# Spectral mixer: the filter's turned sums move from VectorE to accumulating transfers between rows

## The chip, the cores and the metric

The kernel runs on one core of a Trainium2 chip. The metric is the time of one launch on the device, in microseconds (us); lower is better. Five engines work side by side: TensorE (PE in the profile; its weight loads are PEld), VectorE (DVE), ScalarE (ACT), GpSimd (POOL) and SyncE (SP). SP and POOL start most of the transfers here; each works through its own list in order.

## The reference

```python
def _A_ref(x, w_r, w_i):                      # a filter in the frequency domain
    X = jnp.fft.rfft2(x, axes=(-2, -1)) * (w_r + 1j * w_i)
    return jnp.fft.irfft2(X, s=(S, D), axes=(-2, -1))

def _B_ref(x, w1, b1, w2, b2):                # an MLP over the token axis
    h = _layernorm(x, axis=-1)
    u = _gelu(jnp.einsum("bsd,sf->bdf", h, w1) + b1)
    y = jnp.einsum("bdf,fs->bds", u, w2) + b2
    return y.transpose(0, 2, 1)

xn = _layernorm(x, axis=-1)
return x + _A_ref(xn, A_w_r, A_w_i) * _silu(_B_ref(xn, B_w1, B_b1, B_w2, B_b2))
```

Here S = 2048 tokens, D = 512 channels and F = 1792 hidden units, all in float32.

## The kernel before, in words

The rows are cut into 16 blocks of 128 (`NJ`), the hidden units into 14 blocks of 128 (`NF`). A float32 factor is split into a high and a low part, and a product is made of three matmuls (`mm3`): high by high, high by low, low by high. The high part is a ScalarE copy, the low part a VectorE subtraction (`split`, `high_low`).

**The first stage** (to 99.4 us) runs over the 16 row blocks: layernorm, seven of the hidden blocks (in seven PSUM banks), and the filter's first transform, folded into `ey`.

**The middle stage** does two things in turns. One is the other seven hidden blocks, in two batches over the 16 row blocks: 32 parts of `w1` in all, part `i` with four blocks of hidden units where `i` is under 16 and with three above (`BATCHES`, `w1_part`, `hidden_rest`). Six parts are prepared in the first stage (`w1_early`). Of the others, those in `ADDED` (10, 12, ... 20) get their low part without VectorE: ScalarE writes minus the high part, and an accumulating transfer on POOL's queue (`accum_op=ALU.add`) adds `w1` to it once more. The other thing is the filter, eight pairs of frequency groups in the order 1, 2, 0, 3, 4, 5, 6, 7 (`filter_pair(n)`, called o0 to o7 here by place). A pair goes through these steps:

1. `gf` is loaded; eight matmuls by `cd` and a ScalarE copy to `sh`.
2. Eight matmuls of 64x512 (`ps<-sh,gf`), the pair's spectrum in PSUM. ScalarE copies it to `here` (half of `xc`, two copies, L540). Four transfers on SP's queue put into `there`, the other half, the rows of the partner frequency (rows r and r+32 change places, L543).
3. VectorE makes the two turned sums, `here` plus or minus `there` with the row's sign (L561, L562), and multiplies by the filter's weights `wt` (two of 128x1024, L565). `wt` comes by POOL's queue into three buffers (`WT`), so that its loads wait for L565 of the pair before.
4. VectorE adds and subtracts the products (L567 to L569) and puts in the edge columns (L570).
5. 64 small matmuls (`ps<-hf,xc`) transform back; ScalarE copies the result to `ey` (L586).

`PACE` and `LAST` are written out by hand: how many steps of the hidden blocks (three matmuls of 128x512) stand between the filter's steps on TensorE. The step-5 matmuls of pair k come ahead of the step-2 matmuls of pair k+2, so that a pair has about two pair periods from one to the other. TensorE's order is kept as written (`Kept`); the other engines' orders are set by a scheduler, unless an instruction is wrapped in `keep`. Between the filter's steps stand the `forms` of the hidden units: sums and high/low splits for the last stage.

**The last stage** multiplies by `w2` with seven products in place of eight (`ORDER`, `w2_forms`), does the filter's last transform (`channels`, `spectral`), the gate (L789) and the sum into the output.

Of the kernel before, what the change touches and what calls it, by code (L numbers as in the profile page):

```python
# [8 lines left out]
F32 = mybir.dt.float32  # L9
# [20 lines left out]
ADDED = range(10, 22, 2)  # L30
# [21 lines left out]
def _constants():  # L52
# [29 lines left out]
    g = np.zeros((P, 8, 2, 2, 32))  # L82
# [3 lines left out]
    for lo in range(16):  # L86
        for hi in range(4):
            k1, (n, l), (t, h) = 16 * hi + lo, divmod(lo, 2), divmod(hi, 2)
            for r in range(16):
# [15 lines left out]
                p = l * 64 + h * 16 + r, l * 64 + 32 + h * 16 + r  # L105
                for s in range(2):
                    g[rows, n, l, s, h * 16 + r] = back[n, t, p[s], 0] = out[s, rows]
                    freq[p[s], n, t] = k[s]
# [11 lines left out]
        "c_h": back.reshape(16, P, 2, 64).astype(np.float32),  # L120
# [15 lines left out]
def spectral_mixer_kernel(tc, x, w1, b1, w2, b2, wk, we, wx, c_f, c_ft, c_d, c_i, c_g, c_h, out):  # L136
# [14 lines left out]
    with tc.tile_pool(name="ps", bufs=1, space=PSUM) as psp, ExitStack() as left, ExitStack() as right:  # L151
# [9 lines left out]
        for row in range(0, P, 32):  # L161
            sign = 1.0 if row % 64 else -1.0
            G.memset(turn[row:row + 32, 0:1], sign)
            G.memset(turn[row:row + 32, 1:2], -2.0 * sign)
# [14 lines left out]
        w1p = pool(lstage, "left", "w1", 4)  # L179
        lnp = pool(rstage, "right", "ln", 2)  # L180
# [86 lines left out]
        def w1_load(j, f0, nf, up, wide):  # L267
            raw = up.tile([P, wide * P], F32, name=f"w1r{f0}_{j}", tag="w1r", bufs=3)
            SY.dma_start(raw[:, :nf * P], w1[:, j, f0 * P:(f0 + nf) * P])
            return raw[:, :nf * P]  # L270
# [21 lines left out]

        def gelu(ft, bank):
# [3 lines left out]
            A.activation(raw[i][:, half], ps[:, bank], AF.Gelu_apprx_tanh, bias=b1t[:, ft:ft + 1])  # L297

        def high_low(tile, k, src):

            t = tile.rearrange("p k (a c) -> p k a c", a=2)[:, k]
            A.activation(t[..., 0, :], src, AF.Copy)
            V.tensor_sub(t[..., 1, :], src, t[..., 0, :].bitcast(F32))  # L303
# [5 lines left out]
        def forms(i):  # L309
            u = raw[i].rearrange("p a (b c) -> p (a b) c", b=2)  # L310
# [5 lines left out]
            high_low(d[0], d[1], u[:, 2])  # L316
            form[i] = {1: (d[0], d[1])}
            yield
            a = held_tile(f"fa{i}")
            high_low(a, slice(0, 2), u[:, 0:2])  # L320

            V.tensor_sub(u[:, 1], u[:, 1], u[:, 3])
            V.tensor_sub(u[:, 3], u[:, 2], u[:, 3])
            V.scalar_tensor_tensor(u[:, 2], u[:, 1], -1.0, u[:, 2], op0=ALU.mult, op1=ALU.subtract)
            V.scalar_tensor_tensor(u[:, 0], u[:, 2], -1.0, u[:, 0], op0=ALU.mult, op1=ALU.subtract)
            form[i].update({2: (a, 0), 3: (a, 1)})
            yield
            b, c = held_tile(f"fb{i}"), held_tile(f"fc{i}")
            high_low(c, slice(0, 2), u[:, 2:4])
            high_low(b, slice(0, 2), u[:, 0:2])  # L330
            form[i].update({4: (b, 0), 7: (b, 1), 6: (c, 0), 5: (c, 1)})
# [7 lines left out]
        BATCHES = ((((4, 2), (10, 2)), (7, 2, 0, 1)), (((6, 1), (12, 2)), (7, 0, 1)))  # L339
        w1_early, pairs = {}, {}  # L340

        def w1_runs(i, where, queue, **how):
            f = 0
            for f0, nf in BATCHES[i // NJ][0]:
                queue.dma_start(where[:, f:f + nf * P], w1[:, i % NJ, f0 * P:(f0 + nf) * P], **how)  # L345
                f += nf * P

        def w1_early_load(i):
            if i % 2 == 0:
                pairs[i // 2] = usp.tile([P, 2, D], F32, name=f"w1e{i}", tag="u")  # L350
            w1_runs(i, pairs[i // 2][:, i % 2], SY)
# [58 lines left out]
        for j in range(NJ):  # L410
# [10 lines left out]
            if j == 4:  # L421
                SY.dma_start(cd, c_d)
                G.dma_start(cft, c_ft)
            if j in (6, 8, 10, 12):
# [48 lines left out]

        def w1_part(i):
# [3 lines left out]
            j, (runs, _) = i % NJ, BATCHES[i // NJ]  # L478
            n = sum(r[1] for r in runs) * P
            w = w1p.tile([P, 4 * P], F32, name=f"w1s{runs[0][0]}_{j}", tag="w1r", bufs=3)[:, :n]  # L480
            w1_runs(i, w, SY)
# [403 lines left out]
```

## Time and profile before

| | |
|---|---|
| median of 3 runs | 388.89 us (388.51 to 389.69) |
| the profiled execution | 389.42 us, of which 387.6 us are the span of the profile |
| busy: TensorE, VectorE, ScalarE, POOL | 373.5, 317.4, 227.0, 85.5 us |
| moved by transfers | 69.81 MB, mean 180 GB/s |
| granted TensorE clock | 0.994 |

The profile is of one execution. Its own time is 0.5 us above the median, and 1.8 us of it lie outside the span. A row of a timeline gives start, duration, engine, line, operation, tiles and shape; in brackets stands the idle time of the engine just before it, and what ended that. POOL's rows for a transfer are the time of issuing it. A DMA "share" is the time that packets took, over 16 DMA engines.

### The profile page before, as it was taken

What the parts mean: (1) busy time and instruction counts of PE and PEld (TensorE: products, weight loads), DVE (VectorE), ACT (ScalarE), POOL (GpSimd) and SP (SyncE); (2) the same over time, 40 slices, a digit from 0 to 9 for tenths busy, and PEclk for the clock granted to TensorE, in tenths of its full rate; (3) what the DMA queues carried; (4) which work ended last, traced back from release to release, by engine and by line L of the source; (5) the groups of instructions that cost most, each with busy time, mean ns of one, the idle gap of its engine ahead of it and who ended that gap; (6) DMA issues with size and microseconds to landing.
All of it is one profiled execution on the core that took longest, in us unless ns stands there. A gap on an engine that the chain in (4) does not pass through costs nothing.

```text
span 387.6 us, 7793 instructions
## 1 busy us (share of the span) xinstructions
PE 373.5 (96%) x2872; PEld 328.1 (85%) x2872; DVE 317.4 (82%) x671; ACT 227.0 (59%) x411; POOL 85.5 (22%) x147
## 2 busy tenths in 40 slices
PE   7999999999999999999799889999999999999993
PEld 3888888888877777777588889999999999999992
DVE  5899999976549999778996898796969787878871
ACT  4676767754853555575427794655656565646441
POOL 2133233221504444422101003030302020201100
PEclk9999999999999999999999999999999999999997
DMA  8974687312835699988739298997969697876502
GB/s 257 290 262 150 230 275 256 96 55 68 245 95 160 169 268 261 220 234 218 199 94 225 58 261 201 246 183 194 192 159 218 141 222 133 221 147 163 84 1 54
DMA packets 37062, 69.81 MB, mean 180 GB/s; under 512 B 5136, under 2 KB 20896, under 8 KB 36896
## 3 DMA queue, kind: packets, MB, share of 16 engines
q1 hardware_dynamic: 28512, 48.13, 40.7%
q0 software_dynamic: 8512, 21.18, 28.3%
q8 instruction: 22, 0.36, 0.4%
q14 instruction: 16, 0.13, 0.1%
HBM read 60.91 MB, written 8.13 MB: 178 GB/s over the span
## 4 chain that ended last, share of the span: by engine, by line
PE 82%; DVE 5%; DMA 4%; ACT 3%; issue 2%; SPq 2%; POOL 0%; DVEq 0%; ACTq 0%; POOLq 0%
PE ps L823 33%; PE ps L378 20%; PE ps L133 18%; PE ps L242 4%; PE ps L758 3%; DMA s<-in_w_dram 3%; DMA xc<-xc 2%; PE ps L367 2%; PE ps L148 1%; PE ps L147 1%; PE ps L149 1%; ACT w2f L701 1%; SPq L543 1%; DVE xc L565 1%; SPq L345 1%
## 5 line engine op out<-in xcount | busy, mean ns | idle before, releaser
L378 PE MATMUL ps<-h,w1h 128*128 128x512 f32 x224 | 58.7, 398 | 0.0
L133 PE MATMUL ps<-h,w1h 128*128 128x512 f32 x152 | 48.8, 402 | 0.0
L702 DVE TENSOR_TENSOR w2f<-s,w2f 128x896 fp32r<-128x896 f32 x32 | 34.8, 1092 | 16.7 <-ACT w2f L701 16.1
L378 PEld LDWEIGHTS ps<-h,w1h 128*128 128x128 f32 x224 | 40.9, 188 | 7.9
L823 PE MATMUL ps<-fa,w2f 128*128 128x256 f32 x336 | 43.4, 282 | 0.0
L823 PE MATMUL ps<-fc,w2f 128*128 128x256 f32 x336 | 41.7, 280 | 1.6 <-DVE fc L303 0.7
L823 PE MATMUL ps<-fb,w2f 128*128 128x256 f32 x336 | 42.6, 281 | 0.1
L823 PEld LDWEIGHTS ps<-fa,w2f 128*128 128x128 f32 x336 | 41.6, 188 | 0.8
L823 PEld LDWEIGHTS ps<-fc,w2f 128*128 128x128 f32 x336 | 40.3, 188 | 2.2 <-DVE fc L303 0.9
L823 PEld LDWEIGHTS ps<-fb,w2f 128*128 128x128 f32 x336 | 40.5, 188 | 0.5 <-DVE c L793 0.5
L692 POOL DMA_DIRECT2D s<-in_w_dram x16 | 13.9, 870 | 122.3 <-DVE es L763 42.2
L701 ACT ACTIVATE w2f<-s 128x896 fp32r<-128x896 f32 x32 | 30.1, 949 | 15.1 <-DVE s L715 11.0
L133 PEld LDWEIGHTS ps<-h,w1h 128*128 128x128 f32 x152 | 27.2, 188 | 9.8 <-issue 4.9
L702 DVE TENSOR_TENSOR w2f<-a,w2f 128x896 fp32r<-128x896 f32 x24 | 26.1, 1086 | 8.6 <-ACT w2f L701 8.6
L378 PE MATMUL ps<-h,w1l 128*128 128x512 f32 x112 | 30.6, 389 | 0.0
L701 ACT ACTIVATE w2f<-a 128x896 fp32r<-128x896 f32 x24 | 22.8, 951 | 12.6 <-PE ps L823 7.7
L133 PE MATMUL ps<-h,w1l 128*128 128x512 f32 x76 | 29.7, 390 | 0.0
L378 PEld LDWEIGHTS ps<-h,w1l 128*128 128x128 f32 x112 | 21.0, 188 | 4.6
L799 POOL DMA_DIRECT2D out_dram<-g x15 | 13.6, 904 | 43.9 <-DVE g L797 28.4
L373 DVE TENSOR_TENSOR w1l<-w1r,w1h 128x512 fp32r<-128x512 f32 (+1 forms) x32 | 20.7, 648 | 2.4 <-ACT w1h L370 2.2
L597 POOL DMA_DIRECT2D wt<-in_wk_dram x16 | 10.3, 645 | 49.6 <-DVE xc L565 49.0
L823 PE MATMUL ps<-fd,w2f 128*128 128x256 f32 x168 | 21.2, 279 | 0.0
(129 smaller groups left out, 769.4 us busy)
## 6 DMA issues: line engine op xcount, KB each, us to landing
a<-in_w_dram SPq DMA_DIRECT2D x24, 448.0 KB, 3.9
s<-in_w_dram SPq DMA_DIRECT2D x16, 448.0 KB, 4.1
s<-in_w_dram POOLq DMA_DIRECT2D x16, 448.0 KB, 6.6
wt<-in_wk_dram POOLq DMA_DIRECT2D x16, 384.0 KB, 4.9
w1s<-in_w_dram SPq DMA_DIRECT2D x36, 128.0 KB, 3.3
w1r<-in_w_dram SPq DMA_DIRECT2D x16, 256.0 KB, 3.7
xc<-xc SPq DMA_DIRECT2D x32, 128.0 KB, 3.2
x<-in_x_dram SPq DMA_DIRECT2D x15, 256.0 KB, 3.9
```

What stands on the lines that cost most here:

```text
L133: return lambda *args, **kw: self.keep(operation(*args, **kw))
L242: T.matmul(z[:, b], h[:, b * P:(b + 1) * P], c, start=True, stop=True)
L367: T.matmul(ps[:, 0], wz[:, :P], wz, start=True, stop=True)
L373: keep(V.tensor_sub(dst, src, hi.bitcast(F32)))
L378: T.matmul(ps[:, bank + i], w[wi][:, i * P:(i + 1) * P], hj, start=first and j == 0, stop=last and j == NJ - 1)
L597: G.dma_start(wt[:, :3], wk[:, i, 1:])
L692: G.dma_start(t, w2_half(*added), accum_op=ALU.add)
L701: A.activation(wf[:, 0], v, AF.Copy)
L702: V.tensor_sub(wf[:, 1], v, wf[:, 0].bitcast(F32))
L758: T.matmul(pe[:, b % 2, b // 2], yt[:, b], ci[:, b], start=True, stop=True)
L799: G.dma_start(out[:, j, cols], g[:, cols], accum_op=ALU.add)
L823: T.matmul(o, wf[:, wi, i], ui, start=m + a == 0 and n in (1, 2, 5), stop=m == NH - 1 and a == 2, skip_group_check=n in (6, 3, 7, 4))
```

## The change

In the filter, the spectrum is now laid out so that partner frequencies lie in neighbouring rows. ScalarE copies it three times (six copies of 128x512 a pair): times the row's sign into a new tile `tx` (with one buffer), and as it is and with a minus into the two halves of `xc`. Two accumulating transfers on POOL's queue, of 64 rows each, then add the neighbour's row of `tx` to both halves. So VectorE makes no turned sum. The product with `wt` is cut into four of 128x512, and the edge columns take one small operation more. The order of transfers on POOL's queue is fixed: a `wt`, the two accumulating transfers, the next `wt`; `wt` is one transfer in place of two, and so is `hf`.

No `w1` part is made by accumulation: all 26 go through `split`. Raw parts are loaded into pools of their own, up to two or three buffers ahead (`w1_ahead`, `AHEAD`). `turn` is loaded and not made by memsets. At the seam of the middle and last stages the order is written out by hand (`step`, `last_sum`, `form_a` to `form_d`): the first two `w2` tiles are loaded by POOL and split ahead of the last three hidden blocks, and the forms of hidden units 5 and 6 are put between these.

```diff
             xc = mp.tile([P, 2, 2, 2, 256], F32, name=f"xc{n}", tag="xc")
-            there, here = xc[:, 0], xc[:, 1]
+            tx = mp.tile([P, 2, 2, 256], F32, name=f"tx{n}", tag="tx", bufs=1)
+            minus, here = xc[:, 0], xc[:, 1]
...
+            def copies(to, scale):
+                for t in range(2):
+                    A.activation(to[:, :, t].rearrange("p s (g c) -> p g s c", c=64), signals(ps[:, 6 - t]), AF.Copy, scale=scale)
+
+            copies(tx[:, ::-1], turn[:, 1:2])
+            copies(here, 1.0)
+            copies(minus, -1.0)
...
+            wt = wts.pop(), weights(2 * n + 1)
+            for c in range(2):
+                turned_rows = tx[1 - c::2].rearrange("p s t c -> p (s t c)").unsqueeze(1).broadcast_to([64, 2, 2 * D])
+                keep(G.dma_start(xc[c::2].rearrange("p k s t c -> p k (s t c)"), turned_rows, accum_op=ALU.add))
+            if n != order[-1]:
+                wts.append(weights(2 * order[order.index(n) + 1]))
+            yield
+            s1 = mp.tile([P, 3, 2, 2], F32, name=f"s1_{n}", tag="s1")
+            k1, k2 = (e[:, 2 * n:2 * n + 2].rearrange("p t s -> p s t") for e in (e1, e2))
+            V.tensor_mul(s1[:, 0], tx[:, ::-1, :, 0], k2)
+            V.scalar_tensor_tensor(s1[:, 1], tx[:, ::-1, :, 0], turn[:, 0:1], here[:, :, :, 0], op0=ALU.mult, op1=ALU.add)
+            V.tensor_mul(s1[:, 2], s1[:, 1, ::-1], k1)
             for t in range(2):
-                A.activation(here[:, ::-1, t].rearrange("p s (g c) -> p g s c", c=64),
-                             ps[:, 6 - t].rearrange("p (g s c) -> p g s c", s=2, c=64), AF.Copy)
-            for to, of in ((0, 32), (32, 0), (64, 96), (96, 64)):
-                SY.dma_start(there[to:to + 32], here[of:of + 32])
+                V.tensor_mul(here[:, :, t], here[:, :, t], wt[t][:, ::3])
+                V.tensor_mul(minus[:, :, t], minus[:, :, t], wt[t][:, 1:3])
+            yield
+            V.tensor_add(minus, minus, here[:, ::-1])
+            V.tensor_sub(here[:, 0], minus[:, 1], minus[:, 0])
+            V.tensor_add(here[:, 1], minus[:, 1], minus[:, 0])
+            V.tensor_add(here[:, :, :, 0], s1[:, 0], s1[:, 2])
...
-            V.scalar_tensor_tensor(av, bv[:, ::-1], turn[:, 0:1], av, op0=ALU.mult, op1=ALU.add)
-            V.scalar_tensor_tensor(bv, bv, turn[:, 1:2], av[:, ::-1], op0=ALU.mult, op1=ALU.add)
-            for t in range(2):
-                v = xc.rearrange("p k s t c -> p (k s) t c")[:, :, t]
-                V.tensor_mul(v, v, wt[t])
...
         def weights(i):
             wt = mp.tile([P, 4, 256], F32, name=f"wt{i}", tag="wt", bufs=WT)
-            G.dma_start(wt[:, :3], wk[:, i, 1:])
-            G.dma_start(wt[:, 3], wk[:, i, 0])
+            keep(G.dma_start(wt, wk[:, i]))
...
-            if i in ADDED:
-                A.activation(wh, w, AF.Copy)
-                A.activation(wl, wh.bitcast(F32), AF.Copy, scale=-1.0)
-                w1_runs(i, wl, G, accum_op=ALU.add)
-                return wh, wl
             split(wh, wl, w)
...
+        nxt = {"a12": w2_load("a12", w2p, 0, 1, queue=G), "a11": w2_load("a11", w2p, 0, 0, queue=G)}
+        in_order.append(True)
...
         ready = [next(wforms), next(wforms)]
-        run(rest)
-        for steps in zip(forms(5), forms(6)):
-            pass
+        last_sum(12, 1, 0)
+        gelu(12, 0)
+        form_d(5)
+        form_a(5)
+        sums(5)
+        last_sum(13, 2, 1)
+        gelu(13, 1)
+        form_d(6)
+        last_sum(6, 0, 7)
+        form_c(5)
+        form_b(5)
+        ready.append(next(wforms))
+        gelu(6, 7)
+        form_a(6)
...
```

On ScalarE, in the middle stage, this stands around the copies of o3 and o4 (pairs 3 and 4) before. `xc_1766` and `xc_1889` are the two pairs' `xc`, `w1h` and `w1l` a part's high and low half; a row's bracket lists the semaphores it waits for (DMAHW: a transfer started by SP, DMASW: one started by POOL).

```order
L540 ACTIVATE xc_1766<-ps 128x4x2x64 [waits DMAHW1_49,DMAHW2_49,DMAHW0_49,DMAHW3_49,DVE_49,PE_49]
L540 ACTIVATE xc_1766<-ps 128x4x2x64 [waits PE_49]
L484 ACTIVATE w1h_12_1782<-w1s_12_1779 128x512 [waits PE_49]
L485 ACTIVATE w1l_12_1783<-w1h_12_1782 128x512 [waits PE_49,Activation_49]
L144 ACTIVATE w1h_13_1824<-w1s_13_1821 128x512 [waits DMAHW4_49,DMAHW3_49,PE_49]
L525 ACTIVATE sh_0_1819<-ps 128x512 [waits PE_49]
L525 ACTIVATE sh_1_1838<-ps 128x512 [waits PE_49]
```

And now, at the same place (`tx_1770` and `xc_1769` are those of o3):

```order
L582 ACTIVATE tx_1770<-ps,turn 128x4x2x64 [waits DMASW0_49,DVE_49,DMASW7_49,PE_49,Activation_49]
L582 ACTIVATE tx_1770<-ps,turn 128x4x2x64 [waits PE_49]
L582 ACTIVATE xc_1769<-ps 128x4x2x64 x4
L145 ACTIVATE w1h_1786<-w1s_1670 128x512 [waits DMAHW4_49,DMAHW3_49,PE_49]
L145 ACTIVATE w1h_1823<-w1s_1709 128x512 [waits DMAHW6_49,DMAHW5_49,PE_49]
L560 ACTIVATE sh_0_1821<-ps 128x512 [waits PE_49,Activation_49]
L560 ACTIVATE sh_1_1847<-ps 128x512 [waits PE_49,Activation_49]
```

Two copies have become six, and the first of them waits for two transfers that POOL started: those that accumulate from `tx` for the pair before, since `tx` has one buffer.

On POOL's queue, around the same pairs, before (`wt` in two transfers each, and the accumulating transfers of w1 parts 12 and 14):

```order
L597 DMA wt_1717<-in_wk_dram 128x768
L598 DMA wt_1717<-in_wk_dram 128x256
L597 DMA wt_1773<-in_wk_dram 128x768
L598 DMA wt_1773<-in_wk_dram 128x256
L345 DMA w1l_12_1783<-in_w_dram 128x256 x2
L597 DMA wt_1840<-in_wk_dram 128x768
L598 DMA wt_1840<-in_wk_dram 128x256
```

And now (`xc_1769` is o3's, `xc_1897` o4's):

```order
L643 DMA wt_1655<-in_wk_dram 128x1024
L643 DMA wt_1777<-in_wk_dram 128x1024
L598 DMA xc_1769<-tx_1770 64x2x1024 x2
L643 DMA wt_1781<-in_wk_dram 128x1024
L643 DMA wt_1905<-in_wk_dram 128x1024
L598 DMA xc_1897<-tx_1898 64x2x1024 x2
```

Each pair's two accumulating transfers, of 512 KB each, now stand behind a load of `wt` that waits for VectorE's products of the pair before.

More of the change, by code (lines that the diff above doesn't have):

```diff
@@ L104, in _constants @@
                 rows = slice(64 * t, 64 * t + 64)
-                p = l * 64 + h * 16 + r, l * 64 + 32 + h * 16 + r
+                p = [l * 64 + 2 * (h * 16 + r) + c for c in range(2)]
                 for s in range(2):
-                    g[rows, n, l, s, h * 16 + r] = back[n, t, p[s], 0] = out[s, rows]
+                    g[rows, n, l, h * 16 + r, s] = back[n, t, p[s], 0] = out[s, rows]
                     freq[p[s], n, t] = k[s]
@@ L472, in spectral_mixer_kernel, with w1_ahead @@
             folds = fold(j, first_copy(j, z))
+        loaded = {}
+        w1_stage = ExitStack()
+        w1_raw = []
+        def w1_ahead(i):
+            n = BATCHES[i // NJ][1] * P
+            if i == NJ:
+                w1_stage.close()
+                w1_raw[0] = pool(lstage, "left", "w1b", 3)
+            loaded[i] = w1_raw[0].tile([P, n], F32, name=f"w1s{i}", tag="w1s")
+            last = w1_runs(i, loaded[i])
+            if i == 2 * NJ - 1:
+                keep(last)
         def w1_part(i):
@@ L615, in hidden_rest @@
         def hidden_rest():
-            w = w1_parts
+            w, ahead = w1_parts, list(range(NE, 2 * NJ))
             for i in range(2 * NJ):
```

195 lines of the change are left out of this document (105 added, 90 removed).

## The prediction, made before the changed kernel ran

> **What bounds the kernel now.** I read first the page's busy times and its slices, then TensorE's waits, then TensorE's timeline around the filter, then the other engines there.
>
> ```profile
> PE 373.5 (96%) x2872; PEld 328.1 (85%) x2872; DVE 317.4 (82%) x671; ACT 227.0 (59%) x411; POOL 85.5 (22%) x147
> PE   7999999999999999999799889999999999999993
> DVE  5899999976549999778996898796969787878871
> ```
>
> TensorE is busy for 373.5 of 387.6 us. The change leaves its list of matmuls as it is, so all that can be won lies in the 14.1 us in which it is idle, and only where the change reaches: not the start, nor the end. TensorE's timeline shows the places (the bracket is the idle time ahead of a row):
>
> ```profile
> 106.70 1.09 PE L133 MATMUL ps<-sh,gf 64*64 64x512 f32 x8
> ...
> 145.83 1.43 PE L133 MATMUL ps<-hf,xc 64*64 64x64 f32 x62 [0.30 <-DVE xc L574]
> ...
> 167.75 1.16 PE L133 MATMUL ps<-hf,xc 64*64 64x64 f32 x64
> ...
> 178.56 1.16 PE L133 MATMUL ps<-hf,xc 64*64 64x64 f32 x64
> ...
> 190.41 1.16 PE L133 MATMUL ps<-hf,xc 64*64 64x64 f32 x64 [2.72 <-issue]
> ...
> 202.65 1.16 PE L133 MATMUL ps<-hf,xc 64*64 64x64 f32 x64
> ...
> 220.07 0.50 PE L823 MATMUL ps<-fc,w2f 128*128 128x256 f32 x2 [0.69 <-DVE fc L303]
> ...
> 222.66 0.51 PE L823 MATMUL ps<-fc,w2f 128*128 128x256 f32 x2 [0.30 <-ACT w2f L701]
> 223.78 2.50 PE L823 MATMUL ps<-fc,w2f 128*128 128x256 f32 x19 [0.62 <-DVE w2f L702]
> ...
> 228.06 0.50 PE L147 MATMUL ps<-ch,cft 128*128 128x512 f32 x1 [0.63 <-ACT ch L144]
> ```
>
> The filter costs TensorE 0.30 + 2.72 = 3.02 us, the seam with the last stage 0.69 + 0.30 + 0.62 + 0.63 = 2.24 us. Together 5.26 us: this is the most that the change can win. A filter pair takes 178.56 - 167.75 = 10.81 us of TensorE's time. The table by windows says who is late:
>
> ```profile
> 180.00:190.00 10.00, 7.69 (x38) 5.55 (x30) 10.00 (x16) 3.83 (x8) 1.09 (x2) 1.00 0.77 204
> 190.00:200.00 10.00, 9.59 (x101) 8.08 (x102) 9.87 (x16) 5.05 (x10) 0.00 (x0) 1.00 0.29 83
> 130.00:170.00 40.00, 39.70 (x456) 30.91 (x455) 33.99 (x52) 21.31 (x39) 17.82 (x26) 1.00 1.00 251
> ```
>
> The columns are TensorE, its weight loads, VectorE, ScalarE, POOL, the granted clock, the DMA share and GB/s. Around the 2.72 us VectorE is busy for 19.87 of 20 us: it is what TensorE waits for. But from 130 to 170 us the DMA share is 1.00: there the transfer engines are full.
>
> **VectorE and ScalarE.** The groups by line give the durations:
>
> ```profile
> L561 DVE SCALAR_TENSOR_TENSOR xc<-xc,turn 128x1024 f32<-128x1024 f32 x8 | 10.2, 1277 | 0.0
> L562 DVE SCALAR_TENSOR_TENSOR xc<-xc,turn 128x1024 f32<-128x1024 f32 x8 | 10.3, 1284 | 0.2
> L565 DVE TENSOR_TENSOR xc<-xc,wt 128x1024 f32<-128x1024 f32 x16 | 18.9, 1221 | 0.2
> L567 DVE TENSOR_TENSOR xc<-xc 128x1024 f32<-128x1024 f32 x8 | 9.8, 1220 | 0.0
> L568 DVE TENSOR_TENSOR xc<-xc 128x512 f32<-128x512 f32 x8 | 5.5, 684 | 0.1
> L570 DVE TENSOR_TENSOR xc<-s 128x4 f32<-128x4 f32 x8 | 1.3, 158 | 0.1
> L144 DVE TENSOR_TENSOR w1l<-w1s,w1h 128x384 fp32r<-128x384 f32 (+1 forms) x20 | 12.0, 604 | 4.4 <-DMA w1s<-in_w_dram 2.7 <-ACT w1h L144 1.7
> ```
>
> A pair loses 1.28 + 1.28 us of turned sums; its two products of 1.22 us become four of 0.68 (+0.3), and it gains one small operation (0.16). That is 2.1 us less a pair, 17 us in all, less six more splits of 0.60 (3.6 us): VectorE is rid of some 13 us. If it stays the engine that ends last, the 3.02 us go. ScalarE's price is in its timeline:
>
> ```profile
> 108.78 1.08 ACT L540 ACTIVATE xc<-ps 128x512 f32<-128x512 f32 x2
> ```
>
> Two copies take 1.08 us, each further one 0.48, so six take 3.0 us. With 227 of 387 us busy ScalarE can bear 16 us more; but these copies now stand at the head of the filter's chain, not beside it.
>
> **The accumulating transfers.** They carry 2 x 512 KB a pair, which no row of before shows. The nearest rows are the plain transfers between rows that they replace, and the accumulating transfers into SBUF from memory:
>
> ```profile
> xc<-xc SPq DMA_DIRECT2D x32, 128.0 KB, 3.2
> ```
> ```profile
> L692 POOL DMA_DIRECT2D s<-in_w_dram x16: 851/870/895, 206.5 to 355.5; - x16
> ...
> DMA to landing us min/median/max: 5.1/6.6/8.0
> ```
>
> 448 KB accumulated land 5.1 us after the start of their issue at the least, 6.6 in the median. What part of it grows with size is in the queue's share, from 206.5 to 215 us, where nothing but two such transfers is on POOL's queue (packets, MB, share of 16 engines):
>
> ```profile
> q0 software_dynamic: 288, 0.92, 68.9%
> ```
>
> 8.5 us x 0.689 / 0.92 MB = 6.4 us for a MB. So 448 KB (0.459 MB) are 2.9 us of data, and 5.1 - 2.9 = 2.2 us are fixed. A pair's 1.05 MB are then 6.7 us of data. A source in SBUF can make it cheaper or dearer. From 110 to 114 us the plain transfers between rows are alone on SP's queue:
>
> ```profile
> q1 hardware_dynamic: 192, 0.52, 59.2%
> ```
>
> 4 us x 0.592 / 0.52 MB = 4.6 us for a MB without any accumulation. The whole of SP's queue, nearly all of it loads from memory, is cheaper, 0.407 x 387.6 us / 48.13 MB = 3.3 us for a MB:
>
> ```profile
> q1 hardware_dynamic: 28512, 48.13, 40.7%
> ```
>
> So nothing says that SBUF as a source is cheap. If the difference of 1.3 us comes on top of the accumulating 6.4, the data are 1.05 x 7.7 = 8.1 us. I take 7.2 us, nearer to the accumulating row, with 4.6 x 1.05 = 4.8 us (accumulation free) and 8.1 us as bounds. From the first issue to the second landing a pair then takes X = 2.2 + 7.2 = 9.4 us, with bounds of 7.0 and 10.3.
>
> The Trainium skill, "DMA: Bandwidth & Descriptors", section "Anatomy of one DMA — SWDGE (gpsimd) path", gives a GpSimd transfer 2.0 us plus its bytes over 436 GB/s; by that rule 1.05 MB would be an estimated 4.4 us and the time that of the first rival below. The trace disagrees for accumulating transfers: the rule would give 448 KB 3.1 us, and the fastest of 16 took 5.1.
>
> **The new wait.** `tx` has one buffer. ScalarE's first copy for pair k+1 waits until both accumulating transfers of pair k have landed and VectorE has read `tx` (one small operation). ScalarE's list is in order: behind it are queued the high parts of `w1`, the `sh` copies and the gelus, for which TensorE waits. So the pairs form a loop: six copies (3.0), issue and landing (X), and VectorE's operation with three hand-overs (0.16 + 3 x 0.1 = 0.45): 3.45 + X = 12.85 us a pair. TensorE needs one every 10.8. Its place can be worked out from the start. The copies for o0 begin as before at 108.78 (its `gf` matmuls at 106.70 depend on nothing changed), so o0 lands at 108.8 + 3.0 + 0.1 + 9.4 = 121.3, and o7, seven loops on, at 211.25.
>
> From a landing to the back transform VectorE has four products (2.7), three sums (1.22 + 2 x 0.68), four small ones (0.6) and mostly one split (0.6): 6.5 us, and in a stream each of these twelve is some 0.08 shorter, with a hand-over at each end: 5.8 us. So o7's back transform begins at 217.05, in place of 202.65: 14.4 us later, that is a stall of 14.4 + 3.0 = 17.4 us spread over the filter. VectorE's savings do not help, since it waits for the transfers.
>
> POOL's own list adds nothing to the loop: the `wt` load ahead of the accumulating pair waits for VectorE's first two products after the landing (some 1.7 us), and ScalarE's copies take longer.
>
> **The rest.** In the page of transfers the accumulated parts of `w1` are these:
>
> ```profile
> w1l<-in_w_dram POOLq DMA_DIRECT2D x9, 128.0 KB, 5.5
> ...
> w1l<-in_w_dram POOLq DMA_DIRECT2D x3, 64.0 KB, 4.9
> ```
>
> The six accumulated `w1` parts (1.38 MB) and 4.2 MB of plain row transfers leave the queues, 8.4 MB of accumulation come: at 6.4, 4.6 and 6.4 us a MB some 26 us of all 16 engines more, in a stretch that is full from 130 to 170 us. In a loop of 12.85 us there is just room for it; I add nothing for the middle, and up to 1 us a pair for the high end. The earlier `w1` loads and the merged `hf` and `wt` loads are worth what SP and POOL save in issue, which TensorE doesn't wait for: nothing. At the seam, TensorE coming late gives the other engines time, and the forms of units 5 and 6 are put between the last hidden blocks. I take all of the 2.24 us off; if the cover isn't there (the accumulated `s` of the first product 5, which must land within 13 us of the last back transform), none of it goes.
>
> **The sum.** 14.4 - 2.2 = 12.2 us on the profiled execution's 389.42: 401.6, and on the median, which is 0.5 lower, 401.1 us. With X at 8.5 it would be 394, at 10.3 and without the gain at the seam 411: this is the likeliest case's own range, 394 to 411. The time moves by 8 us for each us of X, and comes out even at X = 7.9.
>
> **The rivals.**
> *The transfers keep pace (faster).* If X is 7.2 us or less, o7 is back at 199.6, which is 202.65 less both filter stalls, TensorE never waits in the filter, and all of 5.26 us is won: 383.6 us. It decides at X = 7.9 (even) and 7.2 (all won), so at 5.0 us of data a pair or less in place of 7.2. For it: plain transfers of 128 KB between rows land in 3.2 us, and the low bound of 4.8 us of data lies there. Against it: the 6.4 us a MB. This is also what the skill's rule quoted above would give.
> *The gains cancel.* X between 7.8 and 8.05: 389 us within a measurement's doubt.
> *The DMA engines are the bound.* The share of 1.00 from 130 to 170 us with another 26 us of work stretches X beyond 10.5: 412 us and more. Against it: in the longer loop the demand is spread.
> *The change is small.* X from 8.05 to 8.5: 390 to 394.
>
> **Chances and range.** The likeliest case 0.54; all won 0.31; cancelled 0.05; small loss 0.04; beyond 411 0.06. A measurement of this kernel tells some 0.3% from nothing: faster by more 0.31, the same 0.05, slower 0.64. The range from 384 to 412 leaves out half of the first rival and nearly all of the third, some 0.2.
>
> **What would show it.** Right: ScalarE idle ahead of the `tx` copies until a transfer into `xc` ends; back transforms on TensorE some 12 to 13 us apart, each with 1 to 3 us of idle time ahead; VectorE no longer full at 180 to 200 us; the two transfers landing 9 to 10 us after the first issue. Wrong: landings within 7 us, no idle time ahead of the back transforms, or a stall that ends with a `w1` split in place of the filter.

## The result, and the profile after

The changed kernel takes 411.32 us in the median (410.64 to 412.99, 4 runs), the kernel before 388.75 us beside it: a ratio of 1.058, 95% interval 1.054 to 1.062. That is 22.6 us slower; 12.2 were forecast. The time lies just beyond the likeliest case's own range (394 to 411 us) and inside the wide one (384 to 412). The profiled execution has a span of 408.9 us. One execution of a later experiment (528.46 us, at a granted clock of 0.658 in place of 0.98) is left out of that experiment's median.

The page's busy times and slices, after (TensorE, VectorE, the clock granted to TensorE):

```profile
PE 378.0 (92%) x2872; PEld 329.1 (80%) x2872; DVE 304.8 (75%) x683; ACT 239.8 (59%) x437; POOL 83.4 (20%) x129
PE   8999999999979499778986889999999999999994
DVE  5899999964735762665757688988887878787973
PEclk9999999999998799999999999999999999999999
```

TensorE's idle time went from 387.6 - 373.5 = 14.1 us to 408.9 - 378.0 = 30.9 us, 16.8 more. Its busy time for the same 2872 matmuls rose too, by 4.5 us. Together these are the 21.3 us of span, and both lie in the filter: from o7's back transform (224.30 us, below) to the end are 184.6 us, and before, from 202.65, 184.95. VectorE is rid of 317.4 - 304.8 = 12.6 us, as forecast (some 13).

TensorE's waits, after, from 100 to 232 us (total, times, longest):

```profile
PE ps L134 <- ACT xc L582: 10.2, 5, 3.2
PE ps L134 <- DVE ey L593: 5.3, 1, 5.3
PE ps L134 <- ACT w1h L145: 3.6, 3, 1.8
PE ps L134 <- DVE xc L614: 1.5, 1, 1.5
PE ps L134 <- DVE w1l L145: 1.4, 1, 1.4
```

And its timeline, where these waits stand, with o7's back transform and the seam:

```profile
123.08 1.16 PE L134 MATMUL ps<-cd,ey 128*128 128x128 f32 x8 [3.18 <-ACT xc L582]
140.35 2.05 PE L134 MATMUL ps<-cd,ey 128*128 128x128 f32 x8 [5.28 <-DVE ey L593]
...
166.47 1.16 PE L134 MATMUL ps<-cd,ey 128*128 128x128 f32 x8 [2.78 <-ACT xc L582]
...
224.30 1.16 PE L134 MATMUL ps<-hf,xc 64*64 64x64 f32 x64 [1.47 <-DVE xc L614]
...
245.32 1.16 PE L825 MATMUL ps<-cd,yt 128*128 128x128 f32 x8 [2.03 <-ACT yt L818]
250.47 2.42 PE L890 MATMUL ps<-fa,w2f 128*128 128x256 f32 x19 [0.39 <-DVE w2f L747]
```

The largest stalls are ahead of the forward transforms (`ps<-cd,ey`) of the pair after the one that is moved: these write PSUM banks 6 and 5, which ScalarE's six copies (line 582) must have read first, and the copies wait for a landing. One stall is of another kind: 5.28 us for VectorE's edge products (line 593). The eight matmuls behind it take 2.05 us, where they take 1.16 behind the stall of 3.18: there the clock fell only afterwards (below).

One round of the loop, from the timelines of POOL, VectorE and ScalarE put in order of time:

```profile
111.16 2.06 POOL L598 DMA_DIRECT2D xc<-tx  x2 [10.20 <-ACT xc L582]
119.99 0.22 DVE L605 SCALAR_TENSOR_TENSOR s<-tx,turn,xc 128x4 f32<-128x4 f32 x1 [4.04 <-DMA xc<-tx]
120.30 1.27 ACT L582 ACTIVATE tx<-ps,turn 128x512 f32<-128x512 f32 x2 [1.31 <-DVE s L605]
121.45 2.06 ACT L582 ACTIVATE xc<-ps 128x512 f32<-128x512 f32 x4
124.09 2.05 POOL L598 DMA_DIRECT2D xc<-tx  x2 [1.74 <-ACT xc L582]
```

From the first issue of o0 to VectorE's first read behind the landing: X = 119.99 - 111.16 = 8.83 us; from there to the next issue 4.10 us (a hand-over of 0.31, copies of 3.21, another hand-over of 0.58). VectorE waits for the landing and ScalarE for VectorE: the loop through `tx`, as foreseen, at 12.93 us. VectorE's first reads of the other pairs (line 605) stand at 132.92, 145.58, 163.30, 176.50, 189.32, 202.08 and 217.72 us: the loops take 12.93, 12.66, 17.72, 13.20, 12.82, 12.76 and 15.64 us. Two of them, o2 to o3 and o6 to o7, are 5 and 3 us too long; these the prediction did not have. In o2 to o3 ScalarE's copies start late, at 149.41 us, since TensorE comes late out of the 5.28 us, and X itself is longer: 163.30 - 152.93 = 10.37 us. In o7 VectorE's read did not wait for a landing: it stands in VectorE's list behind a `w1` split (216.59 us) that had waited 6.20 us for ScalarE.

The windows of after (TensorE, its weight loads, VectorE, ScalarE, POOL, granted clock, DMA share, GB/s):

```profile
140.00:144.00 4.00, 3.65 (x13) 3.29 (x14) 0.26 (x2) 1.23 (x2) 0.00 (x0) 0.50 1.05 165
180.00:200.00 20.00, 18.35 (x222) 13.92 (x221) 12.71 (x26) 14.41 (x29) 5.78 (x7) 1.00 0.96 215
```

VectorE is busy for 12.71 of the 20 us in which it was busy for 19.87 before. And TensorE gets half of its clock twice. In windows of half a microsecond the granted clock is 0.50 from 138.1 to 145.0 us, during and behind the wait of 5.28 us, and from 124.5 to 127.9 us, just after the wait of 3.18 us, when its first eight matmuls had already run at the full clock.

### The profile page after: what moved, and what is told of

Read it like the earlier page. It is cut to its first block, busy times and chain, and to the rows that moved or that the text cites. A ratio compares the mean times of both kernels' runs of the same rounds, so it can differ in the third digit from the quotient of the medians.

```text
span 408.9 us, 7752 instructions
## 1 busy us (share of the span) xinstructions
PE 378.0 (92%) x2872; PEld 329.1 (80%) x2872; DVE 304.8 (75%) x683; ACT 239.8 (59%) x437; POOL 83.4 (20%) x129
## 4 chain that ended last, share of the span: by engine, by line
PE 42%; DMA 9%; ACT 8%; DVE 3%; issue 2%; POOL 0%; ACTq 0%; SPq 0%; DVEq 0%
PE ps L890 31%; DMA xc<-tx 8%; PE ps L134 4%; PE ps L825 3%; ACT xc L582 2%; ACT tx L582 1%; PE ps L149 1%; DMA w1s<-in_w_dram 1%; PE ps L148 1%; PE ps L150 1%; ACT w2f L746 1%; ACT w1h L145 1%; DVE w2f L747 1%; POOL xc L598 0%; ACT fc L306 0%
## 5 line engine op out<-in xcount | busy, mean ns | idle before, releaser
L134 PE MATMUL ps<-h,w1h 128*128 128x512 f32 x176 | 57.5, 408 | 1.8 <-ACT w1h L145 1.8
L402 PE MATMUL ps<-h,w1h 128*128 128x512 f32 x224 | 58.7, 398 | 0.0
L402 PEld LDWEIGHTS ps<-h,w1h 128*128 128x128 f32 x224 | 40.8, 188 | 8.0 <-DVE h L397 0.2
L134 PEld LDWEIGHTS ps<-h,w1h 128*128 128x128 f32 x176 | 32.1, 192 | 13.0 <-issue 4.9
L134 PE MATMUL ps<-h,w1l 128*128 128x512 f32 x88 | 35.2, 400 | 1.5 <-DVE w1l L145 1.4
L145 DVE TENSOR_TENSOR w1l<-w1s,w1h 128x384 fp32r<-128x384 f32 (+1 forms) x26 | 15.5, 604 | 26.0 <-ACT w1h L145 26.0
L134 PE MATMUL ps<-cd,ey 128*128 128x128 f32 x128 | 19.3, 298 | 15.5 <-ACT xc L582 10.2
L134 PEld LDWEIGHTS ps<-cd,ey 128*128 128x128 f32 x128 | 18.2, 210 | 19.0 <-ACT xc L582 12.3
L402 PE MATMUL ps<-h,w1l 128*128 128x512 f32 x112 | 30.6, 389 | 0.0
L643 POOL DMA_DIRECT2D wt<-in_wk_dram x16 | 14.6, 911 | 55.0 <-DVE xc L608 55.0
```

The costliest lines, as they stand in the source:

```text
L134: return lambda *args, **kw: self.keep(operation(*args, **kw))
L145: return A.activation(hi, src, AF.Copy), V.tensor_sub(lo, src, hi.bitcast(F32))
L402: T.matmul(ps[:, bank + i], w[wi][:, i * P:(i + 1) * P], hj, start=first and j == 0, stop=last and j == NJ - 1)
L643: keep(G.dma_start(wt, wk[:, i]))
```

## The experiments

Three things could make the 22.6 us: the loop through `tx` (and in it the price of accumulation), the edge products, and the `w1` loads, for which ScalarE waited 11.7 us in three waits. Ratios are to the kernel before, on the same chip. X is that of o0 unless it is said otherwise.

**One sum accumulated, the other made by one addition** (the same outputs):

```
-            copies(minus, -1.0)
+            copies(minus, -2.0)
...
-                keep(G.dma_start(xc[c::2]..., turned_rows, accum_op=ALU.add))
+                keep(G.dma_start(here[c::2], tx[1 - c::2], accum_op=ALU.add))
...
+            V.tensor_add(minus, minus, here)
```

> Only one of the two sums is made by accumulation (0.52 MB a pair in place of 1.05); the other is that sum less twice the signal, so ScalarE writes minus two times the signal and VectorE adds once (1.22 us a pair). Theory of the loop (pairs wait for one another through the single buffer tx, 3.45 us plus X, the time from the first accumulating issue to the second landing): the trace has X at 8.8 to 9.3 us for 1.05 MB, so with 2.2 us fixed about 5.6 here; a loop of 9.0 us is under TensorE's 10.8, the waits of ScalarE for landings go, and the time falls to 386 to 392 us. Rival 1 (the six copies on ScalarE, which hold TensorE's banks 5 and 6 for 3.2 us, are the price, whenever the transfer lands): six copies stay, so TensorE still stands 2 to 3 us ahead of each forward transform and the time stays at 400 to 411. Rival 2 (the transfer engines are full): a third of the accumulated work's 27 us share goes, about 400.

It took 394.14 us, ratio 1.014 (1.010 to 1.018): the doubled accumulation, with the loop that it makes, is the price of 17 of the 22.6 us. The time is a little more than expected. The timelines of POOL, VectorE and TensorE:

```profile
110.23 1.75 POOL L597 DMA_DIRECT2D xc<-tx  x2 [9.81 <-ACT xc L582]
115.72 0.23 DVE L604 SCALAR_TENSOR_TENSOR s<-tx,turn,xc 128x4 f32<-128x4 f32 x1 [3.57 <-DMA xc<-tx]
...
135.04 1.74 PE L134 MATMUL ps<-cd,ey 128*128 128x128 f32 x8 [4.97 <-DVE ey L593]
```

X is 5.49 us for 0.524 MB (5.8 to 7.5 in most later pairs). The step from 1.049 MB gives (8.83 - 5.49) / 0.524 = 6.4 us for a MB and 8.83 - 6.69 = 2.14 us fixed. The six copies stayed, and only 2.2 us of waits for them were left, so the first rival falls: the copies cost little when they needn't wait for a landing. What is left is the edge wait, 4.97 us.

**The same transfers without adding** (both sums are left out):

```
-                keep(G.dma_start(xc[c::2]..., turned_rows, accum_op=ALU.add))
+                keep(G.dma_start(xc[c::2]..., turned_rows))
```

> The same transfers with the same bytes and shapes from the same queue, but they overwrite in place of adding: the sums are left out. It prices accumulation alone. If accumulating is what is dear (the prediction's 6.4 us a MB against 4.6 plain): X falls from 8.9 to about 2.2 + 4.8 = 7.0 us, the loop to 10.5 us, just under TensorE's 10.8, and the time to 386 to 393 us. If a transfer from SBUF to SBUF of this size costs the same without adding: X stays at 8.8 to 9.3, the time at 409 to 413. By the rule of 2.0 us plus bytes over 436 GB/s X would be 4.4 us and the time at the lower end of the first.

```profile
111.65 1.19 POOL L598 DMA_DIRECT2D xc<-tx  x2 [10.96 <-ACT xc L582]
116.83 0.23 DVE L605 SCALAR_TENSOR_TENSOR s<-tx,turn,xc 128x4 f32<-128x4 f32 x1 [0.38 <-DMA xc<-tx]
...
135.75 2.05 PE L134 MATMUL ps<-cd,ey 128*128 128x128 f32 x8 [3.20 <-DVE ey L593]
162.69 2.07 PE L134 MATMUL ps<-cd,ey 128*128 128x128 f32 x8 [3.10 <-ACT xc L582]
```

X falls to 5.18 us, lower than expected: less 2.14 fixed, 3.04 us of data or 2.9 us for a MB. Accumulation makes the data 6.69 / 3.04 = 2.2 times as dear, if the fixed part is the same. The packets on POOL's queue say so too: the same 1.57 MB (both transfers and a `wt` load) take 0.795 of 10 us = 7.95 us of all 16 engines in the changed kernel (111 to 121 us), and 0.650 of 7 us = 4.55 us without adding (111 to 118 us). Less an estimated 1.7 us for the `wt` load (at the 3.3 us for a MB of SP's queue before) these are 6.2 and 2.8 us, again a factor of 2.2. The time, 397.33 us (1.023, 1.018 to 1.028), was missed by 4 us and more: two stalls are left, each followed by matmuls at half the clock (2.05 and 2.07 us), and ScalarE waited 10.3 us for `w1` loads. The first of the two stalls is the edge wait again. Ahead of the second, VectorE's first read of o3 (159.53 us) stood in its list behind a `w1` split and not behind a landing.

**Two `tx`**, with two weight tiles in place of three and the weight loads behind the accumulating transfers; and the same order with **one `tx`** as its control:

```
-            tx = mp.tile([P, 2, 2, 256], F32, name=f"tx{n}", tag="tx", bufs=1)
+            tx = mp.tile([P, 2, 2, 256], F32, name=f"tx{n}", tag="tx", bufs=2)
...
-            wt = wts.pop(), weights(2 * n + 1)
             for c in range(2):
...
-            if n != order[-1]:
-                wts.append(weights(2 * order[order.index(n) + 1]))
+            wt = weights(2 * n), weights(2 * n + 1)
```

> tx has two buffers; to make room the weight tiles have two in place of three, and both weight loads of a pair are issued behind its accumulating transfers, so that the transfers wait for no weight buffer on POOL's queue. Theory of the loop: ScalarE's copies no longer wait for the landing of the pair before; what is next is the queue's data, 6.7 us of accumulation and some 3.5 us of weights a pair, about 10.5 us, so TensorE's 10.8 or a little more sets the pace: 388 to 398 us. Rival 1 (transfer engines full: the share of 0.9 at 13 us a pair is 11.7 us of work a pair): a period of 11.7 to 12, 399 to 404 us. Rival 2 (the copies' hold on the banks): 405 to 411.

> The control of the kernel with two tx: one tx as in the changed kernel, but two weight tiles in place of three, and both weight loads of a pair behind its accumulating transfers. If two tx alone did nothing for the time since the transfer engines are full: this takes about what two tx took or a little more, 412 to 418 us. If the weights with two tiles cost what two tx won (then they would land late and VectorE wait for them, as it did for 7.9 us with two tx): 418 to 428 us. If the single tx is no bound at all: 414 us, with the same waits for landings.

With two `tx` 414.44 us (1.067, 1.061 to 1.073), with one 419.29 us (1.078, 1.076 to 1.080). The waits of ScalarE's `tx` copies for landings and VectorE are gone with two. That wins 5 us against the control; the order with two weight tiles had cost 8. The first expectation, 388 to 398, failed; the control came out by its second case (418 to 428, the weights land late). With two `tx`, the page of transfers and the windows from 170 us say what is next:

```profile
wt<-in_wk_dram POOLq DMA_DIRECT2D x16, 512.0 KB, 9.6
w1s<-in_w_dram SPq DMA_DIRECT2D x36, 128.0 KB, 6.2
...
170.00:190.00 20.00, 18.53 (x218) 14.21 (x218) 9.66 (x22) 13.58 (x27) 3.20 (x4) 0.99 0.98 245
190.00:210.00 20.00, 15.56 (x163) 12.22 (x164) 16.02 (x31) 11.86 (x24) 6.37 (x8) 0.95 0.99 217
```

The weights land 9.6 us after their issue (10.2 in the control, 4.6 in the changed kernel): that is the price of the order, which both share. The DMA share is 0.98 and 0.99 (0.90 and 0.87 in the control), and `w1` parts land after 6.2 us (4.7 in the control): with the single buffer gone, the transfer engines are nearly full. In the control ScalarE's `tx` copies waited only 4.7 us for landings and VectorE (12.8 in the changed kernel), so the 5 us are the worth of a second buffer in this order alone. What two `tx` would bring with three weight tiles stays open.

**The edge products from SBUF**: they read `tx` times the sign, not PSUM bank 6.

```
-                    V.tensor_mul(blocks(room(both, to)), signals(ps[both, 6])..., blocks(room(both, b)))
+                    V.scalar_tensor_tensor(room(both, to), tx[both, 1 - signal, 0]..., turn[both, 1:2], room(both, b), ...)
```

> The four products of the edge column of pair 0 read the signal from tx in SBUF (times the sign, once more) in place of the PSUM bank, so TensorE's next forward transform needn't wait for them. In the changed kernel it waited 5.28 us there, behind a landing and VectorE's whole chain of the pair before, and the clock granted in that stretch was 0.83. Theory (this wait and the slow clock behind it made the loop from o2 to o3 17.7 us where the others take 12.7 to 13.2): the loop of tx goes on at its 12.9 us, so 4 to 5 us go: 406 to 408 us. Rival (the wait only covers one that comes anyhow, as w1 loads are late): 410 to 412 us.

> One look at the kernel that has the full accumulation and the edge products from SBUF; it took 408 us. Theory: the wait of 5.3 us for the edge products is gone, the clock in that stretch is back to 1.00 or nearly, but TensorE still stands 2 to 3 us ahead of most forward transforms for ScalarE's copies, and back transforms follow each other 12.7 to 13.2 us apart. Rival: only the releaser's name has changed, and a wait of 4 to 5 us for a copy or a w1 part stands in its place.

408.14 us, ratio 1.049 (1.045 to 1.052): some 3 us less. The execution whose profile is shown took 410.27 us, so the gain is not sharp. Theory and rival both hold in part:

```profile
136.41 1.16 PE L134 MATMUL ps<-cd,ey 128*128 128x128 f32 x8 [2.61 <-ACT xc L582]
151.72 2.08 PE L134 MATMUL ps<-cd,ey 128*128 128x128 f32 x8 [4.93 <-ACT xc L582]
...
148.43 0.63 ACT L145 ACTIVATE w1h<-w1s 128x512 fp32r<-128x512 f32 x1 [5.00 <-DMA w1s<-in_w_dram]
```

The wait at 140 us is 2.61 us now. But a wait of 4.93 us with the slow clock behind it came 15 us later: ScalarE had stood 5.00 us for a `w1` load ahead of o3's copies. So the loop o2 to o3 took 15.98 us in place of 17.72.

**Late `w1` loads taken away**, on top of that: the raw parts of the filter are loaded once for each buffer and used again (later loads, and so a part of the products, are left out).

```
-            loaded[i] = w1_raw[0].tile(...)
-            last = w1_runs(i, loaded[i])
...
+            if i in (NE, NE + 1, NJ, NJ + 1, NJ + 2):
+                loaded[i] = w1_raw[0].tile(...)
+                w1_runs(i, loaded[i])
+                once[i] = loaded[i]
+            else:
+                loaded[i] = once[NE + i % 2 if i < NJ else NJ + i % 3]
```

> The kernel with full accumulation and the edge products from SBUF, and beside that the raw w1 parts of the filter are loaded once for each buffer and used again: the later w1 loads (most of 5.6 MB) and so a part of the products are left out. With the edge products from SBUF two loops were still longer than 12.7 to 13.2 us (15.98 and 15.73), and in both ScalarE waited for w1 loads (5.00 and 1.98 us). Theory (the loop through tx is 12.9 us whenever nothing else is late, and late w1 loads make the rest): eight landings 12.7 to 13 us apart, the last read of tx at 210 to 211 us and its back transform at 216, and the time 401 to 404 us. Rival (the transfer engines are full, so fewer loads shorten every loop): all loops fall to 11.5 to 12.3 us, 393 to 398 us. Rival 2 (w1 loads are late because TensorE is): 407 to 410 us.

400.62 us, ratio 1.028 (1.025 to 1.031), just under the theory's range; both rivals are out. POOL's first and last accumulating pair, and TensorE's waits in the filter:

```profile
110.89 2.06 POOL L600 DMA_DIRECT2D xc<-tx  x2 [11.32 <-ACT xc L584]
...
200.19 2.03 POOL L600 DMA_DIRECT2D xc<-tx  x2 [1.45 <-ACT xc L584]
...
PE ps L134 <- ACT xc L584: 9.1, 5, 3.3
```

Seven loops take 200.19 - 110.89 = 89.30 us, 12.76 each. With 36 and 16 `w1` loads cut to 7 and 3 the loop kept its length, so at this pace the transfer engines don't set it in most pairs; only in o3, where their share was 1.01 to 1.06 from 156 to 164 us of the changed kernel, did X fall, from 10.37 to 9.03 us. o7's back transform starts at 215.77 us; the prediction had 217.05.

**One sum accumulated and the edge products from SBUF, both:**

```
-                keep(G.dma_start(xc[c::2]..., turned_rows, accum_op=ALU.add))
+                keep(G.dma_start(here[c::2], tx[1 - c::2], accum_op=ALU.add))
...
-                    V.tensor_mul(blocks(room(both, to)), signals(ps[both, 6])..., blocks(room(both, b)))
+                    V.scalar_tensor_tensor(room(both, to), tx[both, 1 - signal, 0]..., turn[both, 1:2], room(both, b), ...)
```

> Both edits together: one sum accumulated, the other made by one addition on VectorE, and the four edge products of pair 0 read tx in SBUF. With one sum accumulated X was 5.5 us (110.23 to 115.72) and pairs from the fourth on came 10.8 us apart, which is TensorE's own pace; what was left was the 4.97 us wait for the edge products, with the clock at 0.91 in that stretch behind it. Theory: the loop is out of the way at X = 5.5, and the edge wait is a second mechanism of its own, so 5 to 8 us go against the 394.1 of one sum alone: 386 to 389 us, level with the kernel before. Rival (the edge wait covered w1 parts that come late anyhow): 391 to 394 us.

390.32 us, ratio 1.002 (1.000 to 1.004): theory confirmed in the main (4 us gone), 1 us above its range. With neither mechanism the change is level with before, not ahead of it.

**The accumulation undone, all else of the change kept** (plain transfers of the rows, VectorE makes both sums, the edge products read `here`):

```
-                keep(G.dma_start(xc[c::2]..., turned_rows, accum_op=ALU.add))
+                keep(G.dma_start(minus[c::2], here[1 - c::2]))
...
+            V.scalar_tensor_tensor(here, minus[:, ::-1], turn[:, 0:1], here, op0=ALU.mult, op1=ALU.add)
+            V.scalar_tensor_tensor(minus, minus, turn2[:, 0:1], here[:, ::-1], op0=ALU.mult, op1=ALU.add)
```

> The changed kernel with its accumulation undone: the rows are moved by plain transfers of 0.52 MB a pair, VectorE makes both turned sums (two operations of 1.28 us a pair), ScalarE writes two copies a pair, tx is gone, and the edge products read SBUF. All else of the change stays: all w1 parts split by VectorE, the earlier w1 loads, merged hf and wt loads, the seam. Theory (the accumulation alone is what costs the 22 us): VectorE has the load of before plus six splits of 0.6 us, 321 us; the time is 388 to 393 us. Rival (the w1 parts or their load order lose of themselves): 395 us and more.

387.48 us, ratio 0.997 (0.995 to 0.999), a little better than expected. The rest of the change costs nothing; the loss is the accumulation's and, in the changed kernel, that of the edge products' new place. TensorE's waits from 100 to 232 us:

```profile
PE ps L823 <- ACT yt L816: 1.4, 1, 1.4
PE ps L134 <- ACT sh L562: 1.3, 1, 1.3
PE ps L134 <- ACT w1h L145: 1.1, 2, 0.7
PE ps L134 <- DVE w1l L145: 0.8, 1, 0.8
PE ps L888 <- DVE w2f L745: 0.4, 1, 0.4
```

**The kernel before with no `w1` part accumulated:**

```
-ADDED = range(10, 22, 2)
+ADDED = ()
```

> The kernel before with one thing of the change alone: none of the six w1 parts is made by accumulation, VectorE subtracts them (six times 0.60 us more for it). In the kernel before VectorE was busy for 19.87 of 20 us around the one stall of 2.72 us at 190 us. Theory (VectorE is what TensorE waits for there): that stall grows by 1 to 3 us, 389 to 392 us. Rival (the accumulated parts landed late and caused the stall): 385 to 388 us.

389.48 us, ratio 1.000 (0.998 to 1.002), the lower end of the theory. VectorE's busy time rose from 317.4 to 320.8 us. So this part of the change is free. The stall at 190 us grew only from 2.72 to 2.76 us, but it was not put to the test: the six parts were accumulated between 132 and 177 us, so that the added splits stand ahead of it. There a wait for VectorE grew, from 0.30 to 1.44 us. At the stall itself TensorE starts, before and in this run, 0.1 us after VectorE's last operation on `xc`, which ends at 190.30 and 192.81 us:

```profile
190.15 0.15 DVE L570 TENSOR_TENSOR xc<-s 128x4 f32<-128x4 f32 x1
```
```profile
192.65 0.16 DVE L570 TENSOR_TENSOR xc<-s 128x4 f32<-128x4 f32 x1
...
192.91 1.16 PE L133 MATMUL ps<-hf,xc 64*64 64x64 f32 x64 [2.76 <-issue]
...
PE ps L133 <- DVE xc L574: 1.4, 1, 1.4
```

**Two edits for more, on the kernel with accumulation undone.** More buffers for raw `w1` parts:

```
-        w1_raw.append(pool(w1_stage, "left", "w1a", 2))
+        w1_raw.append(pool(w1_stage, "left", "w1a", 4))
...
-                w1_raw[0] = pool(lstage, "left", "w1b", 3)
+                w1_raw[0] = pool(lstage, "left", "w1b", 5)
```

> The kernel with accumulation undone and the edge products from SBUF, with the room of tx given to the raw w1 parts: four buffers in place of two, then five in place of three. In the kernel without it ScalarE waited 18.6 us in 8 waits for w1 loads, and TensorE in the filter 1.28 us for sh and 1.1 + 0.8 us for w1 parts. Theory (late w1 loads, whose buffers wait for VectorE's splits, are a loss of their own beside the accumulation): these TensorE waits go, 1 to 3 us less than the 387.5 of the kernel without it: 384.5 to 386.5 us. Rival (TensorE's waits for sh and for the last splits come from the order on ScalarE and VectorE): 387 to 388 us.

387.60 us, ratio 0.996 (0.994 to 0.998), the same as without. ScalarE's waits for `w1` loads went (18.6 to 1.7 us), and TensorE's stall at 180 us stayed:

```profile
PE ps L134 <- ACT sh L562: 1.8, 1, 1.8
```

One sum accumulated in the last four pairs only (the turned rows of those as in the first experiment):

```
+HALF = (4, 5, 6, 7)
...
+                if n in HALF:
+                    keep(G.dma_start(here[c::2], tx[1 - c::2], accum_op=ALU.add))
+                else:
+                    keep(G.dma_start(minus[c::2], here[1 - c::2]))
```

> The kernel with accumulation undone and the edge products from SBUF, but in the last four pairs one of the two sums is accumulated (X = 5.5 us, one addition of 1.22 us on VectorE in place of two operations of 1.28). In the kernel without it VectorE was nearly full around the last stalls, from 170 to 210 us, and TensorE waited there for sh (1.28 us) and for w1 parts (1.9 us). Theory (VectorE's load sets these): it is rid of 1.3 us in each of four pairs, and 1 to 2.5 us go against 387.5: 385 to 386.5 us. Rival (six copies on ScalarE hold TensorE's banks 2 us longer, which costs what VectorE saves): 387 to 390 us.

388.81 us, ratio 0.998 (0.996 to 1.000), so the rival: the wait for `sh` shrank to 0.2 us, and 1.8 us for the copies came. They came in one place, where the six copies began late, behind ScalarE's wait of 4.91 us for a `w1` load.

```profile
148.29 0.63 ACT L146 ACTIVATE w1h<-w1s 128x512 fp32r<-128x512 f32 x1 [4.91 <-DMA w1s<-in_w_dram]
...
PE ps L135 <- ACT xc L584: 1.8, 1, 1.8
PE ps L135 <- ACT sh L563: 0.2, 1, 0.2
```

The two kernels with accumulation undone, with and without more `w1` buffers, are level with each other and the fastest of all these, 0.1 to 0.65% ahead of the kernel before; they accumulate no row of the filter.

## Why the prediction came out as it did

- **Direction and mechanism: right.** The loop through the single `tx`, with VectorE's relief worth nothing, is shown by one sum accumulated (17 us gone with X at 5.5) and by the loop alone (400.62 us, where the sum said 401.1). That these two agree to 0.5 us is in part luck, since errors in the sum cancel. The value of 411 comes from other terms, below.
- **X = 9.4 us: 0.6 too high.** It is 8.83, 8.83 and 8.76 us in the first three pairs and 10.37, 9.30, 8.92 and 8.93 us in the next four; where the late `w1` loads were taken away it is 8.7 to 9.2 us throughout. The 2.2 us fixed and 6.4 us for a MB from the accumulating loads came out as 2.14 and 6.4. The term that was mis-sized is the half-way surcharge for SBUF as source, drawn from 4.6 us a MB of plain row transfers: larger plain ones cost 2.9.
- **The Trainium skill's rule** of 2.0 us plus bytes over 436 GB/s ("DMA: Bandwidth & Descriptors", section "Anatomy of one DMA — SWDGE (gpsimd) path"), an estimated 4.4 us here, is near the plain transfers (5.18 with issue and hand-over) and off by half for accumulating ones (8.83).
- **The loop of 12.85 us: right** (12.66 to 13.20 in five of seven; 12.76 when alone), but by luck, since two errors cancel: X was 0.57 us shorter, and the rest 4.10 us in place of 3.45, the hand-over to POOL alone 0.58. With the measured X and the rest as forecast the sum would have given 396.5 us.
- **5.8 us from landing to back transform: right.** In o0, VectorE's last small operation ends at 125.77, 5.78 us after 119.99.
- **Where TensorE waits: wrong.** Idle time was foreseen ahead of the back transforms, 1 to 3 us each, and its absence was named as a sign against the prediction. Only the last two back transforms have any (1.80 and 1.47 us). The rest is ahead of the forward transforms of the second pair after the one that lands, since the late copies hold banks 6 and 5. The sum does not change by it, as the loop is the same.
- **"POOL's own list adds nothing": right.** The wait ahead of each of the eight accumulating pairs ends with ScalarE's copy (1.74 us at 124.09).
- **The edge products: a missing term, 3 to 5 us** (ratio 1.058 to 1.049; 1.014 to 1.002 where one sum is accumulated). The diff moved their operand from `here` to PSUM; VectorE's list has them behind the landing and the whole chain of the pair before, and bank 6 is held until then. The prediction did not cost this edit at all.
- **"The earlier `w1` loads are worth nothing": wrong, 8 us** (ratio 1.049 to 1.028, from 408.14 to 400.62). On SP's queue the raw loads (L368) stand behind `hf` loads (L570), and wait for buffers that VectorE's splits free; some of these waits end with VectorE's last operation behind a landing (L614):

```profile
SPq L570 <- PE ps L134: 17.8, 4, 13.9
...
SPq L368 <- DVE xc L614: 13.9, 4, 4.1
```

  That the loop delays them and they the loop is argued from these rows; no run shows it. Where the loop was gone (accumulation undone) ScalarE waited longer for such loads, 18.6 us in eight waits, and more buffers for them won nothing.
- **TensorE's clock: a missing term.** Its busy time rose by 4.5 us. The two stretches at half clock hold some 8 us of busy time, in which eight matmuls by `cd` take 2.05 us in place of 1.16 and one of 128x512 0.63 in place of 0.39: an estimated 3 of the 4.5 us.
- **The seam's 2.24 us: wrong.** TensorE waits 2.03 + 0.39 us there now. It is no matter of cover: with accumulation undone, 22 us earlier, it is 1.4 + 0.4 us. So the gain is 0.4 us at the most, and no run came near the 383.6 us of "all won": 387.5 us is the best that was seen.
- **VectorE full at 180 to 200 us as what TensorE waits for: borne out by the order of times** (190.30 and 190.41 us before), though no run took work from VectorE in that stretch of the kernel before.
- **The transfer engines as the bound: not at this pace** (fewer loads, same loop but for o3), but they are next in line: with two `tx` their share is 0.98 to 0.99 from 170 to 210 us.

## What to carry to other kernels

When work goes from a busy engine to transfers, write down the loop through each buffer that the transfer reads: copies in, issue, landing, first release, and compare it with the period of the engine that sets the pace; a single buffer can turn a relieved engine into an idle one. Then look up in the diff each operand that changed its place: an operation that now reads PSUM holds the bank for as long as its engine's list makes it wait. And try to halve the bytes before adding buffers: here one accumulated sum in place of two won 17 us, while the second buffer, which took the room of a weight tile, won 5 of the 8 us that this cost.

## What the runs showed of the hardware

- Two accumulating transfers from SBUF to SBUF move 1.049 MB in 6.7 us of data time, the same bytes without adding in 3.0, a factor of 2.2; the two issues take 2.06 us on POOL, in place of 1.19. The Trainium skill, "Collectives: The Full Stack", section "The bandwidth ceiling: the fold count and why AG ≠ RS ≠ AR", says that an adding transfer is slower since it reads two sources where a copy reads one, and has 1.93 measured for it between two collectives; the factor here agrees with that in size, though no run here shows the reads themselves.
- TensorE's granted clock falls to 0.50 behind idle time, for 3.4 or 6.8 us here. In the changed kernel it changes at 124.49, 127.90, 138.14 and 144.97 us (from windows of half a microsecond): the distances are one, three and two times 3.41 us, and in the other slowed kernels they are whole multiples of 3.41 us too. So what counts is how much of one stretch on this grid is idle, not the length of a wait. From 100 to 235 us of the seven kernels that slowed, the clock was 0.50 after each of the 20 stretches with 1.99 us or more of TensorE's waits in it (2.00 us in the one that ends at 124.49), and it never fell after one with 1.90 us or less. The wait of 2.78 us at 166.47 lies across two stretches, with 1.76 and 1.02 us, and left the clock whole; one of 2.12 us in the kernel with the edge products from SBUF lay within one and halved it. That adds to the price of a stall. The Trainium skill, "TensorE: Matmul & The Clock Gate", section "Part 1: The HAM clock gate (the "warmup" mystery)", has the clock halved behind an idle window of some 3.4 us; the runs agree on the half and on the 3.4 us, but some 2 us of idle time in it were enough.
